# Block sums of an attention kernel taken from a second, unduplicated copy of the values

## The chip, the cores and the metric

The kernel runs on one core of a Trainium2 chip. Its time is device microseconds of one execution; a kernel's number is the median of its runs. Traces come from one profiled execution, whose own time is given beside its span.

## The reference

The program is an attention layer followed by a soft mixture of experts. Cut to what matters:

```python
# attention: B, H, S, D = 4, 8, 768, 64; blocks of 32, window 16
k_sum = k.reshape(B, H, nb, 32, D).max(axis=3)      # 24 block maxima of the keys
v_sum = v.reshape(B, H, nb, 32, D).mean(axis=3)     # 24 block means of the values
scores_l = scale * q @ k.T                          # kept where |i - j| < 16
scores_s = scale * q @ k_sum.T + log(32)
a = softmax(concat([scores_l, scores_s]))
x = (a @ concat([v, v_sum])).transpose(...)         # 3072 tokens x 512
# soft mixture: 8 experts, 4 slots each, hidden 1024
logits = x @ phi
slot_input = softmax(logits, over tokens).T @ x     # 32 slots
slot_out[e] = relu(slot_input[e] @ w1[e]) @ w2[e]
out = softmax(logits, over slots) @ slot_out
```

## The kernel before

**Steps.** Attention goes in 24 steps of 256 tokens and four heads: eight groups `hb` (a batch and half of its heads) of three steps each. A step has, in the order in which the program writes them: `norm` of the step before last, `scores` (TensorE, L253), `soft_max` (VectorE L271 adds the mask and takes the minimum, GpSimd L275 subtracts), then for the step before `trans` (TensorE, L286) and `evac` (ScalarE, L291), `soft_exp` (ScalarE, L280), and `values` (TensorE, L309). Every engine takes its instructions in this written order; the semaphores come from the tiles' reads and writes.

**Values with duplicates.** A value tile `v` holds, for each step, four stretches of 96 tokens that overlap by 32 with their neighbours, each with a column of ones; 24 of the 120 rows of a stretch are left free for the block sums. The host lays this out as `vx`; a tile is 520 KB, one a step, from a pool of five buffers, requested by `load_v` four steps ahead (the buffer comes free with `values` of the step before).

**Block sums.** `v_sum(hb)` adds up the values of a group's 24 blocks: 12 products (three tiles, four stretches) of a 120-row indicator (`cs` at `C_IND`) with 256 columns, into four column groups (32 rows each of a PSUM bank). Its further parts copy the sums to SBUF in two halves (L219, L220: a rounded part and the remainder), order them by a product with the selector `sel` (L224), and put them into `vsst` (L229), from where `put_v` (L235, GpSimd) writes them into each step's tile. `V0` to `V7` in the list `PLAN` say in which step each part of it is written; sum `hb` begins in step 3 `hb` (sum 0 in step 0).

**Maxima of the keys.** `k_max` (VectorE, L184) reduces the two key tiles of the next group in four parts: three in the step 3 `hb` + 1, one in the step after.

**Routing and experts.** The parts `X`, `L`, `t`, `D` of `PLAN` transpose x, form the logits, and accumulate the slot inputs, with a running maximum, beside later attention steps. After the last step the list `TAIL` finishes this: `R` combines the four lanes (with the tile `stk`, loaded for it late), `S` writes the slot inputs as `W1ST` (L449) and a reciprocal `rz` (L453, L454), `C1` takes the second part of the token-side softmax (L463 to L471). Then the attention's pools are closed; their eight PSUM banks (`ps_t` 2, `ps_o` 2, `ps_s` 2, `ps_p` 2) become `pf` (4) and `po` (4). The first expert product `hps` (L657) uses 32 weight pieces, the second (L690) another 32, with the output written beside it (L717 to L728).

**Loads.** All loads are issued by SyncE's queue, in written order; an issue waits for its buffer to be free, and for the landing of an earlier load that used the same semaphore. At the end of each step come: q for later steps, k two groups ahead, `LOADS[i]` weight pieces of 512 KB, `v` (from step 20 on the weights after `v`). 28 pieces have buffers of their own, 15 take over buffers of k, q, v and x as attention ends, 21 follow as the first product frees buffers.

Of the kernel before, what the change touches and what calls it, by code (L numbers as in the profile page):

```python
# [9 lines left out]
F32 = mybir.dt.float32  # L10
F32R = mybir.dt.float32r
# [5 lines left out]
B, H, S, D = 4, 8, 768, 64  # L17
NT, DM, NS, NE, DF = B * S, H * D, 32, 8, 1024
NB = S // 32
W = 96  # L20
U = W + NB
HB = 2 * B
TPS = 3
# [12 lines left out]

LOADS = [1, 1, 1, 2, 2, 1, 2, 1, 2, 1, 1, 2, 2, 1, 1, 1, 1, 2, 1, 2, 3, 2, 2, 1]


PLAN = {
# [38 lines left out]
def attention_soft_moe(  # L81
# [2 lines left out]
    kx: bass.AP,  # L84
    qx: bass.AP,
    vx: bass.AP,
    phi: bass.AP,
    w1: bass.AP,
    w2: bass.AP,
# [10 lines left out]
    wa = ctx.enter_context(tc.tile_pool(name="wa", bufs=NWA))  # L100
    kp = ctx.enter_context(tc.tile_pool(name="kp", bufs=4))
    qp = ctx.enter_context(tc.tile_pool(name="qp", bufs=2))
    vp_ = ctx.enter_context(tc.tile_pool(name="vp_", bufs=5))
    xs = ctx.enter_context(tc.tile_pool(name="xs", bufs=NX))
    att = ctx.enter_context(ExitStack())
    wk = att.enter_context(tc.tile_pool(name="wk", bufs=2, side="right"))
# [20 lines left out]
    pieces += [("w2", k) for k in range(32)]  # L127
    wt, slot = {}, {}

    order = ["wa"] * NWA + "vp kp kp vp xs qp vp vp kp kp vp xs xs xs xs".split()  # L130
    NPRE = len(order)

    def load_piece():
        k = len(slot)
        if k == len(pieces):
            return
        slot[k] = slot[k - NPRE] if k >= NPRE else order[k]
        pool = {"wa": wa, "kp": kp, "qp": qp, "vp": vp_, "xs": xs}[slot[k]]
        t = pool.tile([128, 1024], F32, name=f"w{k}", tag=slot[k])
        p = pieces[k]  # L140
        if p[0] == "w1":
            _, e, c = p
            nc.sync.dma_start(out=t, in_=w1[e, 128 * c : 128 * c + 128, :])
        else:
            nc.sync.dma_start(out=t, in_=w2[p[1]])
        wt[k] = t
# [18 lines left out]
    def load_v(i):  # L165
        if i < NSTEP:
            hb, tp = steps[i]
            v = vp_.tile([128, VC], F32, name=f"v{i}", tag="vp")
            nc.sync.dma_start(out=v, in_=vx[hb, tp])
            vt[i] = v.rearrange("p (a t h c) -> p a t h c", a=2, t=2, h=4)  # L170


    kst = {}


# [23 lines left out]

    def v_sum(hb):  # L200
        pv = post_bank()
        for tp in range(TPS):
            v = vt[hb * TPS + tp]
            for tt in range(2):
                for ab in range(2):
                    g = tt * 2 + ab
                    ic = C_IND + 36 * ab + 4 - 2 * tp
                    nc.tensor.matmul(  # L208
                        pv[32 * g : 32 * g + 32, 0:256],
                        lhsT=cs[0:U, ic : ic + 32],  # L210
                        rhs=v[0:U, ab, tt, :, 0:64],
                        start=(tp == 0),
                        stop=(tp == TPS - 1),
                        tile_position=(0, 32 * g),
                    )
        yield

        vp = wk.tile([128, 2, 256], F32R, name="vp", bufs=1)
        nc.scalar.copy(out=vp[:, 0], in_=pv[:, 0:256])  # L219
        nc.vector.tensor_tensor(out=vp[:, 1], in0=pv[:, 0:256], in1=vp[:, 0].bitcast(F32), op=ALU.subtract)  # L220
        yield
        pv = post_bank()
        for n in range(2):
            nc.tensor.matmul(pv[:, 0:256], lhsT=sel, rhs=vp[:, n], start=(n == 0), stop=(n == 1))  # L224
        yield
        n0 = VS[hb % 2]
        st = vsst[n0 : n0 + NB]
        src = pv[n0 : n0 + NB, 0:256].rearrange("p (h d) -> p h d", h=4)
        nc.scalar.copy(out=st[:, :, 0:64], in_=src)  # L229
# [189 lines left out]
    def lanes():  # L419
        pv = post_bank()  # L420
        pr = pv[0:1, 0:128].rearrange("p (g s) -> p g s", g=4)
        nc.tensor.transpose(pv[0:1, 0:128], stat[:, (NQ - 1) % 2 : (NQ - 1) % 2 + 1], ident)
        yield
        fg = wk.tile([1, 160], F32, name="fg", tag="vp", bufs=1)
        gm, f = fg[:, 128:160], fg[:, 0:128].rearrange("p (g s) -> p g s", g=4)
        nc.vector.tensor_reduce(out=gm, in_=pr.rearrange("p g s -> p s g"), axis=AX, op=ALU.min)
        nc.vector.tensor_tensor(out=f, in0=gm.unsqueeze(1).broadcast_to([1, 4, 32]), in1=pr, op=ALU.subtract)
        nc.scalar.activation(out=f, in_=f, func=AF.Exp)
        yield
        pc = post_bank()  # L430
        nc.tensor.matmul(pc[:, 0:1], lhsT=f.rearrange("p g s -> p (g s)"), rhs=one11, start=True, stop=True)
        yield
        R = wk.tile([128, 128], F32, name="R", tag="vp", bufs=1)
        nc.vector.tensor_scalar(out=R, in0=ps["stk"], scalar1=pc[:, 0:1], scalar2=None, op0=ALU.mult)
        ps["R"] = R
        yield
        pz = post_bank()
        nc.tensor.matmul(pz[:, 0:1], lhsT=R, rhs=stat[:, 2:3], start=True, stop=True)
        ps["z"] = pz
# [82 lines left out]
    nc.sync.dma_start(out=cs, in_=cst)  # L522
    self_ = wk.tile([128, 4, 128], F32, name="self_", tag="xt", bufs=4)[:, 0]
    nc.sync.dma_start(out=self_, in_=selx[0])
    for i in range(TPS):
        load_v(i)
    nc.sync.dma_start(out=phi_sb.rearrange("p c s -> p (c s)"), in_=phi)
    load_k(1)
    load_q(1)
    load_v(3)  # L530
    load_v(4)
    make_identity(nc, ident)
    nc.gpsimd.memset(vsst, 32.0)
    nc.gpsimd.memset(one11, 1.0)
# [5 lines left out]
    for i in range(NSTEP):  # L540
        j = i - 1
        before, after = PLAN.get(i, ("", ""))
        if j > 0:
            norm(j - 1)
        scores(i)
        if i == 1:
            parts("V0 V0")
            put_v(0, 1, nc.gpsimd)
        if i % TPS == 2 and i // TPS + 1 < HB:
            k_max(i // TPS + 1, 3)  # L550
        soft_max(i, 0)
        if i == 1:
            put_v(0, 0, nc.vector)
        if j >= 0:
            trans(j, 0)
            evac(j, 0)
            trans(j, 1)
            evac(j, 1)
            if i % TPS == 2 and i // TPS + 1 < HB:
                k_put(i // TPS + 1, nc.scalar.copy)  # L560
        else:
            for _ in range(3):
                nc.tensor.matmul(wm[:, 0:256], lhsT=acc[:, 0:128], rhs=acc[:, 0:256], start=True, stop=True)
        before, _, beside = before.partition("|")
        parts(before)
        soft_exp(i, 0)
        soft_max(i, 1)
        if i % TPS == 1 and i // TPS + 1 < HB:
            k_max(i // TPS + 1, 0, 1, 2)
        parts(beside)  # L570
        if j >= 0:
            values(j, 0)
            values(j, 1)
        soft_exp(i, 1)
        parts(after)
        if i > 0:
            put_v(i, 0, nc.gpsimd)
            put_v(i, 1, nc.gpsimd)
        if i % 2 == 1:
            load_q((i + 1) // 2 + 1)  # L580
        if i % TPS == 2:
            load_k(i // TPS + 2)
        for _ in range(LOADS[i] if i < 20 else 0):
            load_piece()
        if i > 0:
            load_v(i + 4)
        for _ in range(LOADS[i] if i >= 20 else 0):
            load_piece()
    j = NSTEP - 1
# [59 lines left out]

    row_split(0, 4)  # L650
    row_split(4, 2)
    hps = pf.tile([128, 512], F32, name="hps", tag="pf")[:, 0:256]
    for k in range(32):
        _, e, c = pieces[k]
        t = wt[k].rearrange("p (j f) -> p j f", j=4)
# [113 lines left out]
def _constants():  # L769
    cst = np.zeros((128, C_N), np.float32)  # L770
    i = np.arange(64)[:, None]
    j = np.arange(W)[None, :]
    band = (j - i >= 1) & (j - i <= 31)

    mask = np.zeros((2, 64, 4, U), np.float32)
    for n, ok in enumerate((band & (j >= 16), band, band, band & (j < 80))):
        ab = n // 2
        mask[:, :, n, np.where(np.arange(W) < S0[ab], np.arange(W), np.arange(W) + NB)] = np.where(ok, 0.0, NEG)
    cst[:, C_MASK:C_IND] = mask.reshape(128, 4 * U)

    ind = np.zeros((128, 2, 36), np.float32)
    for ab in range(2):
        for n in range(64):
            ind[16 + n + (NB if 16 + n >= S0[ab] else 0), ab, 4 + n // 32] = 1.0
    cst[:, C_IND : C_IND + 72] = ind.reshape(128, 72)
    sel = np.zeros((128, 128), np.float32)
    for n in range(NB):
        for n0 in VS:
            sel[32 * (n // 2 % 4) + 2 * (n // 8) + n % 2, n0 + n] = 1.0
    p = np.arange(128)  # L790
    stk = (p[:, None] % 32 == p[None, :] % 32).astype(np.float32)
    return cst, np.stack([sel, stk])
# [30 lines left out]
```

## Time and profile before

| | |
|---|---|
| median of 3 runs | 195.24 us (194.88 to 196.53) |
| the profiled execution | 194.91 us, span 193.1 us |
| granted TensorE clock, mean over the span | 0.973 |
| TensorE / VectorE / ScalarE / GpSimd busy | 88 / 60 / 48 / 41% of the span |
| moved by DMA | 67.64 MB, mean 350 GB/s |

A page of the profile gives busy time by engine, 40 slices of the span, the chain of work that ended last, followed back from the end, and groups of instructions by line. `out<-in` names the tiles of an instruction. PE is TensorE's matmuls, PEld its weight loads, DVE VectorE, ACT ScalarE, POOL GpSimd, SPq the queue on SyncE that issues loads. A line number is that of the kernel before.

### The profile page before, as it was taken

How to read it: one execution, taken by the hardware profiler on the slowest of the kernel's cores; microseconds unless marked ns; L12 is line 12 of the kernel's file. 1: busy time of each engine (PE TensorE's matmuls, PEld its weight loads, DVE VectorE, ACT ScalarE, POOL GpSimd, SP SyncE). 2: the span in 40 equal slices, each digit the busy share in tenths (PEclk: the TensorE clock that was granted, in tenths of full speed). 3: DMA queues.
4: the chain of work that ended last, by engine and by line, in shares of the span. 5: the costliest groups of instructions: out<-in, count | busy, mean ns of one | idle time of the engine just before them, and what ended most of it. 6: DMA issues, size and time to landing. Idle time of an engine off the chain costs nothing.

```text
span 193.1 us, 7825 instructions
## 1 busy us (share of the span) xinstructions
PE 169.9 (88%) x3163; PEld 128.7 (67%) x3163; DVE 115.1 (60%) x580; ACT 92.1 (48%) x202; POOL 78.7 (41%) x106
## 2 busy tenths in 40 slices
PE   7779899899799999799989999999879997889950
PEld 5537668677658778578856877876636667768720
DVE  2539959749629958868958867657573020143460
ACT  2036657658464775756686475847220031033440
POOL 2048766856645666576666465860010000000000
PEclk9999999999999999999999999999859999999996
DMA  6999999999998899999899976975959999987696
GB/s 211 351 415 418 416 414 417 419 415 413 404 416 342 277 398 418 410 377 354 247 395 392 392 236 238 311 267 204 333 193 316 417 420 415 416 319 303 259 393 260
DMA packets 19331, 67.64 MB, mean 350 GB/s; under 512 B 2144, under 2 KB 2528, under 8 KB 19296
## 3 DMA queue, kind: packets, MB, share of 16 engines
q1 hardware_dynamic: 19296, 67.15, 90.3%
q8 instruction: 25, 0.41, 0.8%
q14 instruction: 10, 0.08, 0.1%
HBM read 60.85 MB, written 6.29 MB: 348 GB/s over the span
## 4 chain that ended last, share of the span: by engine, by line
PE 60%; DVE 11%; issue 8%; DMA 8%; ACT 5%; POOL 3%; SPq 2%; POOLq 0%; ACTq 0%; DVEq 0%
PE o L309 9%; PE hps L657 8%; PE so L690 8%; DMA v<-vx 8%; PE pt L286 7%; PE s L253 6%; PE pp L208 5%; PE op L717 4%; DVE p L271 3%; DVE kh L184 3%; PE pp L399 2%; PE pp L356 2%; POOL p L275 2%; PE pp L340 2%; PE pp L224 1%
## 5 line engine op out<-in xcount | busy, mean ns | idle before, releaser
L275 POOL TENSOR_TENSOR p<-p,m 128x480 f32<-128x480 f32 x48 | 46.3, 986 | 23.3 <-DVE m L271 22.9
L271 DVE CUSTOM_DVE_ANT_0 p<-s,cs 128x120 f32<-128x120 f32 x192 | 41.0, 278 | 4.9 <-PE s L253 3.5
L280 ACT ACTIVATE p<-p 128x480 f32<-128x480 f32 x48 | 29.0, 608 | 21.8 <-POOL p L275 21.6
L235 POOL COPY v<-vsst 24x520 f32<-24x520 f32 x47 | 29.1, 620 | 20.2 <-issue 17.9
L291 ACT COPY ptr<-pt 120x512 f32<-120x512 f32 x48 | 26.5, 588 | 20.8 <-PE pt L286 20.3
L309 PEld LDWEIGHTS o<-v,ptr 120*64 120x64 f32 x736 | 24.0, 137 | 9.6 <-issue 4.1
L309 PE MATMUL o<-v,ptr 120*64 120x65 f32 x736 | 27.4, 225 | 1.7 <-issue 1.2
L286 PE MATMUL pt<-ident,p 128*120 128x128 f32 x192 | 27.3, 280 | 1.2 <-ACT p L280 1.1
L253 PE MATMUL s<-k,q 64*64 64x120 f32 x768 | 25.9, 269 | 2.1 <-DMA q<-qx 1.2
L253 PEld LDWEIGHTS s<-k,q 64*64 64x64 f32 x768 | 20.3, 133 | 6.1 <-issue 1.7
L286 PEld LDWEIGHTS pt<-ident,p 128*120 128x120 f32 x192 | 20.3, 137 | 6.0 <-ACT p L280 3.3
L184 DVE TENSOR_REDUCE kh<-k 128x30 f32<-128x480 f32 (+1 forms) x32 | 16.1, 545 | 3.4 <-DMA k<-kx 3.4
L657 PE MATMUL hps<-w,W1ST 128*32 128x256 f32 x256 | 15.8, 413 | 1.1 <-DVE lt_all L469 1.1
L329 DVE TENSOR_TENSOR x<-o,z 128x512 f32<-128x512 f32 x23 | 15.9, 691 | 0.8
L271 DVE DVE_READ_ACCUMULATOR2_ANT m<- 128x1 f32 x192 | 15.9, 83 | 0.0
L726 DVE COPY ot<-op 128x512 f32<-128x512 f32 x12 | 7.9, 688 | 11.6 <-PE op L717 11.6
L690 PE MATMUL so<-w,W1ST 128*32 128x128 f32 x256 | 13.4, 275 | 1.0 <-issue 1.0
L657 PEld LDWEIGHTS hps<-w,W1ST 128*32 128x32 f32 x256 | 9.2, 119 | 7.6 <-issue 3.1
L208 PE MATMUL pp<-v,cs 120*32 120x256 f32 x192 | 12.6, 384 | 1.9 <-DMA v<-vx 1.1
L690 PE MATMUL so<-w,W2ST 128*32 128x128 f32 x256 | 13.1, 273 | 0.0
L340 PE MATMUL pp<-ident,x 128*128 128x128 f32 x88 | 12.5, 274 | 0.3 <-ACT xt L346 0.3
L346 ACT COPY xt<-pp 128x512 f32<-128x512 f32 x21 | 12.1, 602 | 0.1
(112 smaller groups left out, 181.2 us busy)
## 6 DMA issues: line engine op xcount, KB each, us to landing
w<-w SPq DMA_DIRECT2D x64, 512.0 KB, 8.9
v<-vx SPq DMA_DIRECT2D x24, 520.0 KB, 7.7
k<-kx SPq DMA_DIRECT2D x16, 472.0 KB, 7.6
q<-qx SPq DMA_DIRECT2D x12, 512.0 KB, 7.0
out<-ot SPq DMA_DIRECT2D x10, 512.0 KB, 3.6
out<-ot SPq DMA_DIRECT2D x4, 256.0 KB, 3.4
cs<-cst SPq DMA_DIRECT2D x1, 288.0 KB, 6.2
self__116<-selx SPq DMA_DIRECT2D x1, 64.0 KB, 5.9
```

The source lines that it names most:

```text
L184: nc.vector.reduce_max(out=kh[:, pr, :, n0 : n0 + m], in_=v[:, :, c0 : c0 + 16 * m].rearrange("p j (m k) -> p j m k", k=16), axis=AX,)
L208: nc.tensor.matmul(pv[32 * g : 32 * g + 32, 0:256], lhsT=cs[0:U, ic : ic + 32], rhs=v[0:U, ab, tt, :, 0:64], start=(tp == 0), stop=(tp == ...
L235: eng.tensor_copy(out=v, in_=src)
L253: nc.tensor.matmul(ps_[i, ab][h : h + 64, u, :], lhsT=qt[i // 2][rows, c : c + 64], rhs=kt[hb, pr][rows, k0 : k0 + U], start=True, stop=Tr ...
L271: nc.vector.tensor_tensor_reduce(out=p[:, n, :], in0=ps_[i, ab][:, 2 * tt + pr, :], in1=maskv[:, mk, :], scale=-0.125, scalar=-NEG, op0=AL ...
L275: nc.gpsimd.tensor_tensor(out=p, in0=p, in1=m.unsqueeze(2).broadcast_to([128, 4, U]), op=ALU.subtract)
L280: nc.scalar.activation(out=p, in_=p, func=AF.Exp, scale=-1.0)
L286: nc.tensor.transpose(pt[:, n, :], p[:, n, :], ident)
L291: nc.scalar.copy(out=ptr, in_=ptr_[i, tt])
L309: nc.tensor.matmul(o[64 * ab : 64 * ab + 64, h, :], lhsT=ptr[:, 2 * pr + ab, 64 * (r ^ ab) : 64 * (r ^ ab) + 64], rhs=v[0:U, ab, tt, h, :] ...
L657: nc.tensor.matmul(hps[32 * j : 32 * j + 32, :], lhsT=W1ST[:, c, 28 * e : 28 * e + 32], rhs=t[:, j, :], start=(k == 0), stop=(k == 31), ti ...
L690: nc.tensor.matmul(so[32 * j : 32 * j + 32, :], lhsT=W2ST[i][:, j, 28 * e : 28 * e + 32], rhs=t[:, i, j, :], start=(e == 0 and i == 0), st ...
```

## The change

- The host adds `vox`, the values once, without overlap or ones: for each group six tiles of 128 tokens by 256 columns (four heads), 768 KB. It comes in beside `vx`, which stays.
- `v_sum` makes 6 products of 128 rows from it instead of 12: tiles 0 to 3 go to the four column groups, tiles 4 and 5 to the first two. The indicator is now one pattern of 128 rows; the selector's rows follow the new order of the sums.
- `load_vo(hb)` requests the copy: group 0 ahead of the first value tiles, group 1 in two halves in buffers of the x pool, groups 2 to 7 at the end of steps 3, 6, ..., 18, three steps ahead of their sum, in the single buffer of a new pool `vo`. The SBUF copy of the sums (`vp`) takes turns in the same buffer.
- The value pool has four buffers instead of five, and `v` is requested three steps ahead. `fg` and `R` of the tail take buffers of the softmax pool.
- At the start, the order of the loads after the first k, q and constants is now: copy 0, v 0, v 1, q 1, k of group 1, copy 1, v 2, v 3, phi.
- `LOADS` has 34 pieces instead of 36, and fewer of them early; some entries of `PLAN` move by a step (transposes `X4`, `X10` to `X15`, `D2`).
- `hps` takes its bank from `po`.

```diff
-LOADS = [1, 1, 1, 2, 2, 1, 2, 1, 2, 1, 1, 2, 2, 1, 1, 1, 1, 2, 1, 2, 3, 2, 2, 1]
+LOADS = [0, 0, 1, 1, 1, 1, 1, 2, 1, 1, 1, 1, 2, 1, 1, 1, 2, 1, 1, 2, 3, 4, 3, 2]
...
-    9: ("t0 t0 X4 X4 V3 | V3", "V3 V3 D0 D0"),
-    10: ("X5 X5", ""),
+    9: ("t0 t0 V3 | V3", "V3 V3 D0 D0"),
+    10: ("X4 X4 X5 X5", ""),
...
-    14: ("X9 X9 X10 X10 D1 | D1", ""),
+    14: ("X9 X9 D1 | D1", ""),
...
-    16: ("X11 X11", ""),
+    16: ("X10 X10 X11 X11", ""),
...
-    18: ("t2 t2 X12 X12 V6 | L2 V6", "V6 V6"),
-    19: ("X13 X13 X14 X14 D2 | D2", ""),
-    20: ("X15 X15", "L3 L3"),
+    18: ("t2 t2 V6 | L2 V6", "V6 V6 D2 D2"),
+    19: ("X12 X12 X13 X13", ""),
+    20: ("X14 X14 X15 X15", "L3 L3"),
...
-    vp_ = ctx.enter_context(tc.tile_pool(name="vp_", bufs=5))
+    vp_ = ctx.enter_context(tc.tile_pool(name="vp_", bufs=4))
+    vo = ctx.enter_context(tc.tile_pool(name="vo", bufs=1))
...
-    order = ["wa"] * NWA + "vp kp kp vp xs qp vp vp kp kp vp xs xs xs xs".split()
+    order = ["wa"] * NWA + "kp kp vp xs qp vp vp vo kp kp vp xs xs xs xs".split()
...
+    def load_vo(hb):
+        if hb == 1:
+            halves = [xs.tile([128, 1024], F32, name=f"vo1{n}", tag="xs")[:, 0:768] for n in range(2)]
+        elif hb < HB:
+            whole = vo.tile([128, 1536], F32, name=f"vo{hb}", tag="vo")
+            halves = [whole[:, 0:768], whole[:, 768:1536]]
+            nc.sync.dma_start(out=whole, in_=vox[hb])
+        if hb == 1:
+            for n in range(2):
+                nc.sync.dma_start(out=halves[n], in_=vox[hb, :, 768 * n : 768 * n + 768])
+        if hb < HB:
+            kst["vo", hb] = [halves[t // 3][:, 256 * (t % 3) : 256 * (t % 3) + 256] for t in range(6)]
...
     def v_sum(hb):
         pv = post_bank()
-        for tp in range(TPS):
-            v = vt[hb * TPS + tp]
-            for tt in range(2):
-                for ab in range(2):
-                    g = tt * 2 + ab
-                    ic = C_IND + 36 * ab + 4 - 2 * tp
-                    nc.tensor.matmul(
-                        pv[32 * g : 32 * g + 32, 0:256],
-                        lhsT=cs[0:U, ic : ic + 32],
-                        rhs=v[0:U, ab, tt, :, 0:64],
-                        start=(tp == 0),
-                        stop=(tp == TPS - 1),
-                        tile_position=(0, 32 * g),
-                    )
-        yield
-
-        vp = wk.tile([128, 2, 256], F32R, name="vp", bufs=1)
+        for t in range(6):
+            g = t % 4
+            ic = C_IND + 4 - 4 * (t // 4)
+            nc.tensor.matmul(
+                pv[32 * g : 32 * g + 32, 0:256],
+                lhsT=cs[:, ic : ic + 32],
+                rhs=kst["vo", hb][t],
+                start=(t < 4),
+                stop=(t + 4 > 5),
+                tile_position=(0, 32 * g),
+            )
+        yield
+
+        vp = vo.tile([128, 2, 256], F32R, name="vp", tag="vo")
...
-        fg = wk.tile([1, 160], F32, name="fg", tag="vp", bufs=1)
+        fg = wk.tile([1, 160], F32, name="fg", tag="p", bufs=3)
...
-        R = wk.tile([128, 128], F32, name="R", tag="vp", bufs=1)
+        R = wk.tile([128, 128], F32, name="R", tag="p", bufs=3)
...
-    for i in range(TPS):
-        load_v(i)
+    load_vo(0)
+    load_v(0)
+    load_v(1)
+    load_q(1)
+    load_k(1)
+    load_vo(1)
+    load_v(2)
+    load_v(3)
     nc.sync.dma_start(out=phi_sb.rearrange("p c s -> p (c s)"), in_=phi)
-    load_k(1)
-    load_q(1)
-    load_v(3)
-    load_v(4)
...
+        if i > 0 and i % TPS == 0:
+            load_vo(i // TPS + 1)
...
-            load_v(i + 4)
+            load_v(i + 3)
...
-    hps = pf.tile([128, 512], F32, name="hps", tag="pf")[:, 0:256]
+    hps = po.tile([128, 512], F32, name="hps", tag="op")[:, 0:256]
...
-    ind = np.zeros((128, 2, 36), np.float32)
-    for ab in range(2):
-        for n in range(64):
-            ind[16 + n + (NB if 16 + n >= S0[ab] else 0), ab, 4 + n // 32] = 1.0
-    cst[:, C_IND : C_IND + 72] = ind.reshape(128, 72)
+    cst[np.arange(128), C_IND + 4 + np.arange(128) // 32] = 1.0
...
-            sel[32 * (n // 2 % 4) + 2 * (n // 8) + n % 2, n0 + n] = 1.0
+            sel[32 * (n // 4 % 4) + 4 * (n // 16) + n % 4, n0 + n] = 1.0
```

More of the change, by code (lines that the diff above doesn't have):

```diff
@@ L86, in attention_soft_moe @@
     vx: bass.AP,
+    vox: bass.AP,
     phi: bass.AP,
@@ L137, in load_piece @@
         slot[k] = slot[k - NPRE] if k >= NPRE else order[k]
-        pool = {"wa": wa, "kp": kp, "qp": qp, "vp": vp_, "xs": xs}[slot[k]]
+        pool = {"wa": wa, "kp": kp, "qp": qp, "vp": vp_, "vo": vo, "xs": xs}[slot[k]]
         t = pool.tile([128, 1024], F32, name=f"w{k}", tag=slot[k])
@@ L805 @@
         "vx": vx,
+        "vox": np.ascontiguousarray(
+            inputs["v"].reshape(HB, 4, 6, 128, D).transpose(0, 3, 2, 1, 4).reshape(HB, 128, 6 * 256)
+        ),
         "phi": np.ascontiguousarray(inputs["moe_phi"].reshape(4, 128, NS).transpose(1, 0, 2).reshape(128, 4 * NS)),
```

## The prediction

> **What bounds the kernel now.** First the page: busy times, slices, and the chain of waits by engine and by line.
>
> ```profile
> span 193.1 us, 7825 instructions
> PE 169.9 (88%) x3163; PEld 128.7 (67%) x3163; DVE 115.1 (60%) x580; ACT 92.1 (48%) x202; POOL 78.7 (41%) x106
> ...
> GB/s 211 351 415 418 416 414 417 419 415 413 404 416 342 277 398 418 410 377 354 247 395 392 392 236 238 311 267 204 333 193 316 417 420 415 416 319 303 259 393 260
> ...
> PE 60%; DVE 11%; issue 8%; DMA 8%; ACT 5%; POOL 3%; SPq 2%; POOLq 0%; ACTq 0%; DVEq 0%
> PE o L309 9%; PE hps L657 8%; PE so L690 8%; DMA v<-vx 8%; PE pt L286 7%; PE s L253 6%; PE pp L208 5%; PE op L717 4%; DVE p L271 3%; DVE kh L184 3%; PE pp L399 2%; PE pp L356 2%; POOL p L275 2%; PE pp L340 2%; PE pp L224 1%
> ```
>
> TensorE is busy 88% of the span and makes 60% of the chain. L208, the block sums that are rewritten, is alone 5% of it, 9.7 us. Transfers are 8%, all of `v`; and from the third slice to the twelfth the queue moves 404 to 419 GB/s, which looks like its ceiling. Next the windows by stage (busy time of PE, PEld, DVE, ACT, POOL; then granted clock, DMA share, GB/s), and the chain in order of time (start us, us, what).
>
> ```profile
> 0.00:17.00 17.00, 13.04 (x150) 9.35 (x150) 8.02 (x44) 4.20 (x7) 5.04 (x13) 1.00 0.90 340
> 17.00:58.00 41.00, 36.55 (x721) 28.22 (x716) 28.69 (x171) 25.81 (x55) 26.61 (x35) 1.00 1.02 414
> 58.00:130.00 72.00, 68.93 (x1373) 55.03 (x1370) 55.38 (x310) 46.23 (x103) 46.05 (x59) 1.00 0.91 337
> 130.00:141.30 11.30, 9.03 (x93) 6.25 (x92) 7.95 (x25) 4.55 (x15) 0.00 (x0) 0.86 0.76 276
> 141.30:149.00 7.70, 7.66 (x109) 4.44 (x113) 4.18 (x10) 1.44 (x3) 0.95 (x1) 0.76 0.70 230
> ```
>
> ```profile
> 4.34 7.34 DMA v<-vx
> ...
> 17.26 7.60 DMA v<-vx
> 24.90 0.64 PE pp L208 x8
> ...
> 54.12 1.50 PE pp L208 x24
> ...
> 86.84 1.36 issue
> ...
> 114.57 1.43 PE pp L208 x24
> ...
> 141.34 15.82 PE hps L657 x256
> ```
>
> In the 72 us of steady attention TensorE is busy 96% and VectorE 77%, so I take TensorE as the bound there, and a matmul removed as time saved unless VectorE is next. The two `v` entries are the start (sum 0 wants three tiles) and step 3 (sum 1 wants tile 5, requested only when step 1 freed a buffer).
>
> **The change part by part.** *Sums 1 to 7.* One matmul of the source is two instructions, and four column groups run side by side. From the timeline:
>
> ```profile
> 10.16 0.64 PE L208 MATMUL pp<-v,cs 120*32 120x256 f32 x8
> ...
> 12.50 0.64 PE L208 MATMUL pp<-v,cs 120*32 120x256 f32 x8 [0.72 <-DMA v<-vx]
> ...
> 23.76 1.78 PE L208 MATMUL pp<-v,cs 120*32 120x256 f32 x24
> ```
>
> Eight instructions are two rounds of four groups and last 0.64 us; 24 are six rounds and last 1.50. A round is so (1.50 - 0.64) / 4 = 0.215 us. After, tiles 0 to 3 fill the four groups and tiles 4 and 5 come back to the first two: two rounds and two half-filled ones. I count a half-filled round as a whole one, since its group is busy as long; the bound on the other side is half the price. That is four rounds for six, 0.43 us saved in each of seven sums, 3.0 us (4.5 by the other bound). That the operand has 128 rows instead of 120 should cost nothing; L657's products of 128 rows and as many columns, 64 rounds in 15.82 us and partly at a slow clock, bound a round at 0.247, and the saving from below at 0.30 a sum, 2.1 us. Sum 1 also waited for tile 5: 1.78 against the usual 1.43, so 0.35 more. Where this goes to the end: the sums stand on the chain whole. But every third step VectorE has the maxima of k on top, and the chain's DVE, ACT and POOL entries (19%) show that an earlier TensorE is sometimes held there. I take 80% of 3.35, 2.7 us. The copy of the sums, its difference, the selection matmul and the put into the tiles stay as they are.
>
> *The start.* Ahead of sum 0 there were two k tiles, q, the constants, the selector and three v tiles; the page has the sizes, and the third tile's block began at 12.50.
>
> ```profile
> w<-w SPq DMA_DIRECT2D x64, 512.0 KB, 8.9
> v<-vx SPq DMA_DIRECT2D x24, 520.0 KB, 7.7
> k<-kx SPq DMA_DIRECT2D x16, 472.0 KB, 7.6
> q<-qx SPq DMA_DIRECT2D x12, 512.0 KB, 7.0
> ...
> cs<-cst SPq DMA_DIRECT2D x1, 288.0 KB, 6.2
> self__116<-selx SPq DMA_DIRECT2D x1, 64.0 KB, 5.9
> ```
>
> Now 768 KB of values stand for 1560: 792 KB less, 2.0 us at 414 GB/s, so sum 0 could begin at 10.5. It ends 0.64 + 2 x 0.215 = 1.07 later, at 11.6; before it ended at 13.14. That is 1.5 us. But the k tiles of the second head group slide back. Their second one and its reader:
>
> ```profile
> L157 SPq DMA_DIRECT2D k<-kx x1: 328/328/328, 7.6 to 7.6; - x1
> ...
> DMA to landing us min/median/max: 7.3/7.3/7.3
> ```
>
> ```profile
> 16.35 1.57 DVE L184 TENSOR_REDUCE kh<-k 128x30 f32<-128x480 f32 x3
> ```
>
> It landed at 7.6 + 7.3 = 14.9. Up to it the queue had 3368 + 64 + 944 = 4376 KB; after the change (sum's values, two v tiles, q, k) 5072, 696 KB more, 1.7 us: 16.6. The last of these three reductions needs it; about 0.6 us long, it ended at 17.92 and now cannot end before 17.2. VectorE is in order, and the next step's normalising and softmax queue behind. So the start brings 0.7 us; its bounds are 1.5 if the tile comes sooner, and -0.4 if the queue loses another microsecond, as its 340 GB/s up to 17 us would have it.
>
> *The queue.* Up to the tile `stk`, the last thing the routing tail needs from memory, the old program moves 16 k, 12 q, 24 v, 38 weight pieces and 480 KB of constants, 46,112 KB. The new one moves eight copies of 768 KB more and two pieces less: 51,232 KB, or 52.5 x 10^6 bytes. By 17 us 5.8 are there (340 x 17); the rest takes 112.8 us at 414 GB/s, and `stk` lands at 129.8. It is read at 137.45:
>
> ```profile
> L594 SPq DMA_DIRECT2D stk<-selx x1: 422/422/422, 127.4 to 127.4; - x1
> L434 DVE TENSOR_SCALAR R<-stk,pp x1: 291/291/291, 137.4 to 137.4; 128x128 f32<-128x128 f32 x1
> ```
>
> So the ceiling leaves 7.6 us of gain free at that point. The same for the k tiles of the last head group, which must come after 39.5 x 10^6 bytes: 98.5 at the earliest, against reductions that began at
>
> ```profile
> 104.80 1.57 DVE L184 TENSOR_REDUCE kh<-k 128x30 f32<-128x480 f32 x3
> ```
>
> With a gain of 3 us there it still fits, with about 3 us to spare, but the queue will be full almost throughout, so I charge 0.3 us for late tiles (bounds 0 and 2.5). The trace covers the other moves. Value tiles are asked for three steps ahead instead of four; steps last about 5 us, landing 7.7. The request of a copy waits on SP for the selection matmul of the same step, and behind it stand the weights and the v tile; v waited for the values product of that step already, and the selection follows it by under 1 us.
>
> By the Trainium skill (DMA: Bandwidth & Descriptors, Specifications) HBM gives one core about 358 GB/s; by that `stk` would land at 17 + 46.7 / 0.358 = 147 and the sum would come out near 204 us. The ten slices at 404 to 419 speak against it here.
>
> *The first expert product.*
>
> ```profile
> 139.46 0.29 DVE L449 COPY W1ST<-tl 128x128 f32<-128x128 f32 x1 [1.19 <-issue]
> ...
> 139.97 0.16 DVE L454 RECIPROCAL rz<-rz 128x1 f32<-128x1 f32 x1
> ...
> 140.77 0.42 DVE L469 TENSOR_TENSOR lt_all<-o,kh 128x256 f32<-128x256 f32 x1
> ...
> 141.34 1.93 PE L657 MATMUL hps<-w,W1ST 128*32 128x256 f32 x16 [1.07 <-DVE lt_all L469]
> ```
>
> Its weights are written at 139.75, but it waits for L469, which reads the banks of `ps_o`; the pool `pf` lies over them. In `po`, over `ps_s` and `ps_p`, the last readers are the `rz` lines, done by 140.13. That frees 1.07 us. The granted clock is 0.86 and 0.76 around this place, so the first part of the product is slow. If the slow phase ends when it ended before, an earlier microsecond does half a microsecond's work. I take 0.8 (bounds 0.5 and 1.1).
>
> By the Trainium skill (TensorE: Matmul & The Clock Gate, Part 1) the clock is released after a busy window of about 3.4 us on a grid that runs free of the kernel. By that the term is 0.5 unless the earlier start crosses a window's edge; the rows here show means of the clock and no edges.
>
> *The rest.* Some `X` parts move by a step, out of the steps of sums 3, 4 and 6, and `D2` moves from step 19 to the end of step 18. From the chain:
>
> ```profile
> 105.33 1.06 PE pp L399 x8
> ...
> 109.48 0.44 PE pp L340 x4
> ```
>
> Their number stays, so TensorE's sum does too; the copies of `X` (ScalarE) and the accumulation of `D2` (VectorE) go with them, and `D2` leaves a step with three k maxima on VectorE for one without. The parts `L` that read them are in a later step, except `L3`, which now follows `X14` and `X15` in one step where it followed `X15` alone. I count 0, bounds -0.4 and 0.7, one of these groups falling on or off the chain. `fg` and `R` take slots whose last readers are the transposes of steps 22 and 23, ten microseconds earlier: nothing. TensorE has 192 instructions fewer, which shifts its stalls without a shown cause (86.84, 1.36 us): I count 0, bounds plus and minus 1.4.
>
> Sum: 2.7 + 0.7 + 0.8 - 0.3 = 3.9 us. The profiled execution took 194.91, so 191.0; the median of the three runs, 195.24, is 0.33 above it: **191.3 us**, a case from 189.6 to 192.9.
>
> **The rivals.** *All of it counts*: 3.35 + 1.5 + 1.07 = 5.9, giving 189.3. For it: TensorE at 96%; against it: the late k tile. *VectorE or GpSimd is next in the sum's steps*, and only the start, the wait of sum 1 and half of the expert product remain: 0.7 + 0.35 + 0.5 = 1.6, giving 193.6. For it: the 19% of the chain; against it: the sums are on the chain in every step shown. *The queue becomes the bound, slower*: the place is `stk`, or a k or v tile before it. The point is the rate: 46.7 x 10^6 bytes in 137.45 - 17 us is 388 GB/s; below, routing waits. At 337, the mean of the second window, `stk` would land near 146, 8.7 late: 195.2 + 8.7 - 0.8 = 203; at 375, 199. Against it: that window's 337 is what was asked for, with slices of 418 and 410 in it. *The bank isn't free sooner* because the other pool is held as long: 0.8 less, 192.1.
>
> **How the numbers follow.** Forecast 0.50, all of it 0.13, VectorE next 0.21, queue 0.11, of which nearly all is slower, bank 0.05. The skill's 358 GB/s is in the queue's chance. About 1% is what a measurement of this kernel can tell (the three runs spread 0.8%). Faster by over 1%, below 193.3: 0.50 + 0.13 + 0.05 = 0.68; within 1%: 0.21; slower: 0.11. The range goes from 188.9 to 194.8; it leaves out the queue's case and the ends of the others.
>
> **What would show it.** Right: L208 in groups of 12 instructions of about 1.07 us; no wait of L208 for `v`; a VectorE wait for k near 15 to 17 us; over 400 GB/s up to about 100 us; the expert product about 0.2 us after `rz`. Wrong: `R`, the k maxima or the put waiting for a transfer after 20 us; steps as long as before with TensorE idle in front of VectorE; the slow clock lasting longer than before.

## The result and the profile after

The changed kernel takes 189.0 us in the median of four runs (187.4 to 189.9) against 195.1 beside it: ratio 0.970, interval 0.965 to 0.975, so 6.1 us less (5.8 by the ratio). On a second chip it was 187.7 against 194.9, ratio 0.963 (0.958 to 0.967). The forecast was 191.3, a gain of 3.9 us. The profiled execution took 187.42 us, the fastest of the four, against 194.91 in the trace before, so the two traces show 7.5 us, about 1.4 more than the medians. Executions also differ by stretches of 3.4 or 6.8 us at half clock that fall in different places, so below a ratio carries a time and a trace carries a wait.

Lines have moved by the change: L208 is now L221, L271 L284, L309 L322, L399 L412, L434 L447, L469 L482, L657 L674. The page, by the parts that were read before:

```profile
span 185.6 us, 7677 instructions
PE 167.0 (90%) x3067; PEld 126.1 (68%) x3067; DVE 114.9 (62%) x580; ACT 92.6 (50%) x202; POOL 78.8 (42%) x106
...
GB/s 208 380 416 415 415 415 423 413 419 406 415 415 427 413 411 378 410 418 419 413 419 419 412 418 417 417 417 414 417 402 391 416 414 420 417 410 366 238 422 256
...
PE 47%; DMA 28%; DVE 7%; POOL 7%; issue 5%; ACT 2%; SPq 0%; POOLq 0%; DVEq 0%
```

The windows of the same two stretches:

```profile
17.00:58.00 41.00, 37.39 (x720) 29.61 (x719) 31.28 (x190) 26.13 (x56) 26.92 (x35) 1.00 1.03 415
58.00:130.00 72.00, 69.04 (x1314) 53.91 (x1309) 56.49 (x304) 49.37 (x114) 44.27 (x56) 1.00 1.02 413
```

TensorE has lost 96 matmuls. The second stretch went from 337 to 413 GB/s: the queue now runs at its ceiling from the third slice to the thirty-sixth, 378 to 427 GB/s. DMA's share of the chain went from 8 to 28%. The parts of the forecast can be read in the timeline (first two rows) and in the chain (the others):

```profile
108.63 1.06 PE L221 MATMUL pp<-vo,cs 128*32 128x256 f32 x12
...
16.36 0.66 DVE L200 TENSOR_REDUCE kh<-k 128x30 f32<-128x480 f32 x1
```

```profile
123.58 8.94 DMA stk<-selx
...
132.62 0.30 DVE R L447
132.96 1.92 PE tl L458 x8
...
135.26 0.53 PE o L476 x2
135.78 15.55 PE hps L674 x256
```

A sum lasts 1.06 us (forecast 1.07). The last of the three reductions, which needs the late k tile, ends at 17.02 (forecast: not before 17.2; before the change 17.92). The expert product follows the transposes of `C1` with no wait. But `R` now stands behind the landing of `stk`, at 132.5, which the forecast had put at 129.8.

### The profile page after: what moved, and what is told of

It reads as the page before. It is cut to its first block, busy times and chain, and to the rows that moved or that the text cites. A ratio compares the mean times of both kernels' runs of the same rounds, so it can differ in the third digit from the quotient of the medians.

```text
span 185.6 us, 7677 instructions
## 1 busy us (share of the span) xinstructions
PE 167.0 (90%) x3067; PEld 126.1 (68%) x3067; DVE 114.9 (62%) x580; ACT 92.6 (50%) x202; POOL 78.8 (42%) x106
## 2 busy tenths in 40 slices
DMA packets 20626, 73.92 MB, mean 398 GB/s; under 512 B 2288, under 2 KB 2672, under 8 KB 20592
## 4 chain that ended last, share of the span: by engine, by line
PE 47%; DMA 28%; DVE 7%; POOL 7%; issue 5%; ACT 2%; SPq 0%; POOLq 0%; DVEq 0%
PE hps L674 8%; PE so L707 8%; DMA q<-qx 7%; DMA w<-w 6%; DMA v<-vx 6%; PE pt L299 5%; PE o L322 5%; PE s L266 5%; POOL p L288 5%; DMA stk<-selx 5%; DMA k<-kx 5%; PE op L734 4%; DVE p L284 2%; PE pp L353 2%; POOL v L248 2%
## 5 line engine op out<-in xcount | busy, mean ns | idle before, releaser
L284 DVE CUSTOM_DVE_ANT_0 p<-s,cs 128x120 f32<-128x120 f32 x192 | 41.1, 278 | 4.7 <-PE s L266 3.3
L322 PEld LDWEIGHTS o<-v,ptr 120*64 120x64 f32 x736 | 24.2, 137 | 11.0 <-issue 7.1
L322 PE MATMUL o<-v,ptr 120*64 120x65 f32 x736 | 27.9, 225 | 3.5 <-issue 2.5
L284 DVE DVE_READ_ACCUMULATOR2_ANT m<- 128x1 f32 x192 | 16.0, 83 | 0.0
L674 PE MATMUL hps<-w,W1ST 128*32 128x256 f32 x256 | 15.6, 409 | 0.0
L674 PEld LDWEIGHTS hps<-w,W1ST 128*32 128x32 f32 x256 | 8.2, 118 | 7.3 <-issue 2.1
L353 PEld LDWEIGHTS pp<-ident,x 128*128 128x128 f32 x88 | 10.0, 141 | 0.6 <-ACT xt L359 0.5
```

The costliest lines, as they stand in the source:

```text
L284: nc.vector.tensor_tensor_reduce(out=p[:, n, :], in0=ps_[i, ab][:, 2 * tt + pr, :], in1=maskv[:, mk, :], scale=-0.125, scalar=-NEG, op0=AL ...
L322: nc.tensor.matmul(o[64 * ab : 64 * ab + 64, h, :], lhsT=ptr[:, 2 * pr + ab, 64 * (r ^ ab) : 64 * (r ^ ab) + 64], rhs=v[0:U, ab, tt, h, :] ...
L353: nc.tensor.transpose(pv[:, 128 * c : 128 * c + 128], x, ident)
L674: nc.tensor.matmul(hps[32 * j : 32 * j + 32, :], lhsT=W1ST[:, c, 28 * e : 28 * e + 32], rhs=t[:, j, :], start=(k == 0), stop=(k == 31), ti ...
```

## Experiments

Each ran beside the kernel before on its chip, five rounds. Ratios are to that. The runs are spread over three chips, so kernels of different sets are compared by their ratios.

**1. Six rounds again.**

```diff
-        for t in range(6):
+        for n, t in enumerate((0, 1, 2, 3, 0, 1, 2, 3, 4, 5)):
...
-                stop=(t + 4 > 5),
+                stop=(n < 4 or t + 4 > 5),
```

> The changed kernel (189.0 us), but the first four products of each block sum are made twice, so that a sum takes six rounds of the four column groups again, as before the change; nothing else differs and the queue's loads are the same. TensorE theory (a round removed is time saved, 80% of 8 x 0.43 = 2.7 us): 191.7. Queue theory (the tail now waits 1.3 us for the tile stk, so the first 1.3 us of slower sums are hidden): 190.3. Hidden theory (VectorE and GpSimd set the steps with a sum): at most 189.4.

191.6 us, ratio 0.982 (0.977 to 0.988); the changed kernel has 0.970 and 0.963. Against these two numbers the run costs 2.4 and 3.9 us, each with about 1.5 us either way. The hidden theory falls. The other two are not told apart: TensorE's 2.7 fits both numbers, and the queue theory's 1.3 fits the first. The run doesn't price the rounds alone either, since its trace has more stalls of TensorE than the changed kernel's; they are counted below. The wait for `stk` is gone: `R` now waits for TensorE (second row; the first is the changed kernel on the second chip).

```profile
DVE R L447 <- DMA stk<-selx: 2.0, 1, 2.0
```

```profile
DVE R L447 <- PE pp L444: 0.2, 1, 0.2
```

But `stk` itself landed at 136.8 there (issued at 126.8, 10.0 later), 3 to 4 us after the two traces of the changed kernel: the requests of the copies wait for buffers that the steps free (SyncE waited 27.2 us for the selection product, against 21.4 and 18.2), so slower steps make the queue later too.

**2. The old PLAN in the changed kernel, and the new one in the old.** The diffs are the lines of `PLAN` shown with the change, taken back and put in.

> The changed kernel with the old PLAN: transposes X4, X10, X12 to X15 and D2 stand in their old steps. My forecast costs the moves at nothing: 189.0, within 0.4. Rival: steps 18 and 19 became 2.1 us shorter in the two traces, 0.43 of it the shorter sum; if the moves did the rest, 190.4 or more.

188.8 us, 0.967 (0.962 to 0.973): no difference, as the forecast had it. But in the kernel before:

> The kernel before (195.6 us on the last chip) with the new PLAN alone. Plan theory (two of the steps that lost a transpose or D2 get 1.3 us shorter each, as in the run with plan and bank): 193.0. Forecast (moves cost and bring nothing), so that the 4.4 us of plan and bank came from the bank and the clock behind it: 195.2 or more.

193.0 us, 0.989 (0.984 to 0.994). The moves alone bring 2.2 us (1.2 to 3.2). The list of waits of one line, L399, the product of a part `D`, says where to look. The kernel before, then with the new PLAN:

```profile
its engine sat idle before it (us, times) until:
  ACT xt L346: 3.3, 4
  ACT dsb L391: 0.9, 2
```

```profile
its engine sat idle before it (us, times) until:
  ACT dsb L391: 0.9, 2
  issue: 0.2, 1
```

The list adds up the waits of the matmuls and of their weight loads, which run at the same time; the matmuls alone have 1.4 of the 3.3 us:

```profile
PE pp L399 <- ACT xt L346: 1.4, 2, 1.0
```

Two parts `X` ahead of a `D` take both banks of `ps_p`, and `D` waits until ScalarE has copied one of them out. The timeline of step 14, before and with the new PLAN:

```profile
78.49 1.04 PE L340 MATMUL pp<-ident,x 128*128 128x128 f32 x8
80.55 1.07 PE L399 MATMUL pp<-x,dsb 128*32 128x512 f32 x8 [1.02 <-ACT xt L346]
```

```profile
78.22 0.60 PE L340 MATMUL pp<-ident,x 128*128 128x128 f32 x4
78.75 1.07 PE L399 MATMUL pp<-x,dsb 128*32 128x512 f32 x8
```

With one `X` there the wait of 1.02 us is gone, and the other of 0.4 in step 19 too. So 1.4 of the 2.2 us are seen in rows, within what the times allow; the rest is not accounted for. In the changed kernel with the old PLAN this wait is back, and yet costs nothing measurable (the two measurements of the changed kernel allow up to about 2 us). The trace of experiment 4, which has the old PLAN as well, shows it, and shows that `R` doesn't wait for `stk` there:

```profile
PE pp L412 <- ACT xt L359: 1.6, 2, 1.2
...
DVE R L447 <- PE pp L444: 0.2, 1, 0.2
```

**3. The bank.**

```diff
-    hps = po.tile([128, 512], F32, name="hps", tag="op")[:, 0:256]
+    hps = pf.tile([128, 512], F32, name="hps", tag="pf")[:, 0:256]
```

> The changed kernel with the first expert product in a bank of pf again. By the forecast's term it waits 1.1 us for L482 (the line that was L469) and costs 0.8 (0.5 to 1.1): 189.8. Rival: the slow clock of the product's first part ends at the same time and the product is behind the tile stk anyway: within 0.3 of 189.0.

189.3 us, 0.971 (0.966 to 0.977). The wait is back as foreseen:

```profile
PE hps L674 <- DVE lt_all L482: 1.2, 1, 1.2
```

The time lies between no change and 0.9% over the two measurements of the changed kernel: undecided between the two expectations. The reverse, in the kernel before:

> The kernel before with the first expert product in a bank of po, nothing else. The wait of 1.1 us goes: ratio 0.9945 to 0.9975 (1.1 to 0.5 us). Rival, plan and bank gave 3.9 us together and the moves 2.2, so the bank 1.7: 0.991.

193.9 us, 0.990 (0.981 to 0.999), and the wait of L657 is gone from its list. It brings something, between 0.3 and 3.7 us (the ratio rests on three of the six runs); whether 0.8 or 1.7 these runs can't tell. Both parts together, without the copy:

> The kernel before (195.1 us) with the two parts that need no copy of the values: the new PLAN and the bank in po; sums, loads and buffers are the old ones. My forecast: the bank alone, 0.8 us: 194.3. Rival, the moves of PLAN count 1.4 more: 192.9 or less.

191.3 us, 0.980 (0.974 to 0.986): 3.9 us, about the sum of the two, 2.2 and 1.9.

**4. The copy alone**, the changed kernel with the old PLAN and the old bank.

> The changed kernel with the old PLAN and the old bank: the copy, its sums, the new loads and buffers alone. Queue theory (what these two parts save is mostly spent waiting for the queue): ratio to before 0.970 to 0.975, about 190. Additive theory (moves 2.2 us and bank 1.1 go back in full from 0.966): 0.983, about 192.

189.4 us, 0.975 (0.969 to 0.981): 4.8 us, where the queue theory put it. The additive 0.983 lies just outside; but it starts from 0.966, between the changed kernel's 0.970 and 0.963, and from 0.963 it would be 0.980, inside. Moves 2.2, bank 1.9 and copy 4.8 make 8.9 us one by one; together they make 5.8 and 7.3 on the two chips. That would be 1.6 to 3.1 us lost where they meet, but the intervals add up to about 2.5 us either way, so the times alone don't show a loss. The traces do, under 5.

**5. A lighter queue.**

```diff
-            halves = [xs.tile([128, 1024], F32, name=f"vo1{n}", tag="xs")[:, 0:768] for n in range(2)]
+            halves = [xs.tile([128, 1024], F32, name=f"vo1{n}", tag="xs")[:, 0:768] for n in range(1)]
...
-            nc.sync.dma_start(out=whole, in_=vox[hb])
+            nc.sync.dma_start(out=whole[:, 0:256], in_=vox[hb, :, 0:256])
...
-            for n in range(2):
-                nc.sync.dma_start(out=halves[n], in_=vox[hb, :, 768 * n : 768 * n + 768])
+            nc.sync.dma_start(out=halves[0][:, 0:256], in_=vox[hb, :, 0:256])
...
-            kst["vo", hb] = [halves[t // 3][:, 256 * (t % 3) : 256 * (t % 3) + 256] for t in range(6)]
+            kst["vo", hb] = [halves[0][:, 0:256] for t in range(6)]
```

> The changed kernel with 128 KB of each copy loaded instead of 768 (all six products of a sum read the first 256 columns): left out are five sixths of the values that go into the block sums; instructions of the engines are the same, the queue has 5.2 x 10^6 bytes less, 12.7 us at 414 GB/s. Queue theory: no wait for stk (1.3) and none for the k tile at the start (0.8): 186.9, and 186 or less if a full queue also slows the steps between. Rival, the full queue costs nothing: 189.0 within 0.4.

184.6 us, 0.947 (0.942 to 0.952), against 187.7 for the changed kernel in the same set: 3.1 us (1.7 to 4.4 by the ratios), for the same instructions of the engines. Its two stretches:

```profile
17.00:58.00 41.00, 37.73 (x728) 29.75 (x731) 30.85 (x188) 26.46 (x57) 27.22 (x35) 1.00 0.98 378
58.00:130.00 72.00, 69.36 (x1318) 54.07 (x1318) 56.28 (x303) 49.36 (x115) 43.97 (x56) 1.00 0.99 388
```

The rival falls: the full queue costs something, by the medians 3.1 us, against the 1.3 and 0.8 that I could name. And if it is the queue that hides the moves of PLAN, they must show again here:

> The kernel with 128 KB copies (five sixths of the values left out of the block sums, 184.6 us on the last chip, ratio to before 0.947) with the old PLAN. Queue theory (with the whole copies the moves of PLAN are hidden behind the full queue; without the queue they are worth the 2.2 us that they are worth in the kernel before): ratio 0.958, 186.8. Rival (the shorter sums leave the moves nothing to gain): 0.947, 184.6 within 0.6.

186.3 us, 0.961 (0.954 to 0.967), 0.013 above the same kernel with the new PLAN, 2.6 us. Without the queue's load the moves are worth what they are worth in the kernel before, so the rival falls; with it, nothing measurable.

The traces show where the moves go. GpSimd subtracts twice in each step; the second of these rows is the changed kernel, the first the copy alone, with the old PLAN, both in the last step:

```profile
121.51 1.93 POOL L288 TENSOR_TENSOR p<-p,m 128x480 f32<-128x480 f32 x2 [0.69 <-DVE m L284]
118.56 1.93 POOL L288 TENSOR_TENSOR p<-p,m 128x480 f32<-128x480 f32 x2 [0.67 <-DVE m L284]
```

The same start in eight traces, with the start of `R` and the span (us):

| kernel of the trace | last subtractions | `R` | between | span |
|---|---|---|---|---|
| before | 124.53 | 137.45 | 12.92 | 193.1 |
| before, new PLAN | 122.25 | 135.18 | 12.93 | 191.5 |
| copy alone | 121.51 | 134.43 | 12.92 | 187.5 |
| changed | 118.56 | 132.62 | 14.06 | 185.6 |
| changed, second chip | 119.32 | 134.04 | 14.72 | 186.8 |
| changed, six rounds | 124.55 | 137.47 | 12.92 | 190.1 |
| light copies | 117.96 | 130.88 | 12.92 | 182.9 |
| light copies, old PLAN | 120.90 | 133.82 | 12.92 | 184.8 |

By the last step the moves have brought 2.3 us in the kernel before, 2.9 with the light queue, and 3.0 and 2.2 with the full one (copy alone against the two traces of the changed kernel; the bank, in which they differ too, acts behind `R`). So a full queue does not hide them in the steps. From there to `R` it is 12.9 us, except where `R` waits for `stk`: there 1.1 and 1.8 us are added, and of the moves 1.8 and 0.4 are left. In the copy's own trace `stk` landed at 133.7 and `R` began at 134.4: that was all the room that the moves could use. The six rounds show the same from the other side: 6.0 and 5.2 us later in the last step, 4.9 and 3.4 at `R`.

The same table says what the light queue saves. By the last step it is 0.6 and 1.4 us, and this was there by step 3 (0.8 and 1.3), after the k tile at the start, whose reductions end 0.8 us sooner than in the changed kernel:

```profile
14.65 1.57 DVE L199 TENSOR_REDUCE kh<-k 128x30 f32<-128x480 f32 x3
```

In the steps between, the full queue costs nothing in these traces. The wait for `stk` adds 1.1 and 1.8. Behind `R` another 1.0 and 0.7 remain. There TensorE's clock is at half for 3.4 us with the light copies and for 6.8 in both traces of the changed kernel, worth up to 1.7 us (half of the difference, an estimate). The mean granted clock over the runs agrees, 0.985 against 0.978. So a part of the 3.1 us may be the clock; that the queue causes this isn't shown.

**6. Towards a better version.** First the request of `stk` at the end of step 22:

```diff
+        if i == 22:
+            ps["stk"] = const.tile([128, 128], F32, name="stk", tag="sel")
+            nc.sync.dma_start(out=ps["stk"], in_=selx[1])
```

> The changed kernel with the request of the tile stk moved from behind the weights of the tail to the end of step 22, ahead of seven weight pieces. Queue theory (the tail waits 1.3 us for stk, since the queue is full to that point): stk lands some 8 us sooner, the wait goes, 187.7. Rival (something else in the tail is ready no sooner, or the slow clock gives it back): 189.0 within 0.4.

Beside it the changed kernel once more:

> The changed kernel once more, beside the next three on one chip: 189.0 again, within 0.8.

187.1 us, 0.957 (0.952 to 0.963), beside 187.7, 0.963. The wait of `R` for `stk` was 2.0 us in the second trace of the changed kernel and is gone here:

```profile
  DMA stk<-selx: 2.0, 1
```

```profile
  PE pp L444: 0.2, 1
```

From the last subtractions to `R` it is 12.9 us again (120.08 to 132.99). By the ratios the gain is 1.0 us, less than the wait, and the intervals overlap: not settled. Then the order of the first loads as well:

```diff
     load_v(0)
-    load_v(1)
     load_q(1)
     load_k(1)
+    load_v(1)
```

> The changed kernel with stk requested at the end of step 22, and at the start the second q tile and the two k tiles of group 1 ahead of the second value tile. The k tiles land 1.3 us sooner; VectorE waited 1.2 us for the second of them. Ratio to before 0.953 (stk alone 0.957), 186.0 to 186.5. Rival: the value tile is now late by as much, no gain: 0.957.

186.6 us, 0.961 (0.957 to 0.966), all six runs within 0.7 us. The wait of VectorE for k at the start is gone (first row: `stk` alone; second: with the new order; columns: total, times, longest). That wait was 0.5 us in the changed kernel, with another 0.2 before the reduction of the second tile, not 1.2, which is the time from the start of the first reduction to that of the third (15.19 to 16.36). By time it can't be told from `stk` alone (it ran on another chip).

```profile
DVE kh L200 <- DMA k<-kx: 3.2, 2, 2.7
```

```profile
DVE kh L200 <- DMA k<-kx: 2.6, 1, 2.6
```

Both versions have lower medians than the changed kernel, by 0.3 and 0.6%, and by the ratios 0.5 and 0.1%: neither is clear of the noise.

## Why the forecast was right, and where its size was off

The direction and the range held, and so did the first reason: TensorE was the bound of the steps, and rounds removed were time saved. The size was off, and that it lies as near as it does is partly luck: three terms were missed, and one of them has the other sign. The measured 6.1 lies on the rival in which all terms count (5.9), but not for its reasons: that one had full shares for start and sums, and neither the moves, the stalls nor the queue at their real size.

- *Sums*: 1.06 us each against 1.07, so the row was right. What share of it reaches the end (80% in the forecast) was not measured: experiment 1's 2.4 to 3.9 us hold stalls besides the rounds, and what `R` hides.
- *Start*: the late k tile landed at about 16.4 (issued at 7.5, 8.9 later), forecast 16.6; the reductions ended 0.9 us sooner than before, forecast 0.7. Right, and by its own limit: 1.5 was there for the sum, and VectorE's wait for k took the rest.

```profile
L159 SPq DMA_DIRECT2D k<-kx x1: 328/328/328, 7.5 to 7.5; - x1
...
DMA to landing us min/median/max: 8.9/8.9/8.9
```

- *Expert product*: the wait went as described. Of its 0.8 us the runs leave 0.3 to 3.7; the half-clock argument could not be decided.
- *Moves of PLAN*: costed at nothing, with a bound of 0.7. They measured 2.2 us in the kernel before and 2.6 with a light queue. This is the first mis-sized term. The sum counted their instructions, which stay, and looked at VectorE; it didn't look at what the moved lines wait for. In the old trace the waits of L399's matmuls for ScalarE's copies of `X`, 1.4 us, named the larger part of the price.
- *Stalls of TensorE*: counted at nothing, with a bound of 1.4. "Issue" in the list of waits is idle time for which the profile shows no releaser. TensorE's matmuls before, then after:

```profile
PE pp L356 <- issue: 1.8, 1, 1.8
PE op L717 <- issue: 1.3, 1, 1.3
PE o L309 <- issue: 1.2, 2, 0.8
PE so L690 <- issue: 1.0, 1, 1.0
```

```profile
PE o L322 <- issue: 2.5, 4, 1.0
PE so L707 <- issue: 0.8, 1, 0.8
PE s L266 <- issue: 0.2, 1, 0.2
```

  With 0.2 more at L253 the trace before has 5.5 us of them, the changed kernel's two have 3.5 and 2.5: 2 to 3 us less. It isn't one execution's luck. The four traces with the old sums have 5.5 to 6.8, each with 1.8 to 2.0 at L356 and 1.3 to 1.8 at L717; the nine with the new sums have 2.3 to 3.8 and nothing at these two places; the one with six rounds, which has 64 matmuls more, has 5.3. So the stalls go with the program. Why they come, and what they are worth in time, no run here shows.
- *Queue*: charged at 0.3 with a bound of 2.5. By the light copies its cost is 3.1, of which 0.8 is the k tile, already in the start's term: so 2.3, the clock's part included; the wait for `stk` alone is 1.1 to 1.8. The ceiling was right (414 forecast, 415 and 413 measured), and the bytes moved rose from 67.64 to 73.92 MB, the eight copies. But `stk` landed at 132.5, not 129.8. And the 7.6 us of room were measured against the old time of `R`: as every other term brought `R` forward, it ate its own room. `R` was ready 6.1 us sooner (132.62 less the wait of 1.3, against 137.45) and `stk` came 2.7 later than forecast: 8.8 against 7.6. In the rival of the slower queue the two rates stand on different footings: 337 was put on the second stretch alone, 375 on everything behind 17 us. `R` waiting for a transfer stood on the forecast's list of signs against it, and it did come.

So the forecast missed about 2.2 us of gain by the moves, 2 to 3 us of stalls that went, and 2 us of cost by the queue. Moves and queue largely cancel in the changed kernel; what is left, 2.2 us of 195, is the size of the stalls that went. That the terms add up so is an account from single traces, not a measurement of each. The 358 GB/s of the Trainium skill (DMA: Bandwidth & Descriptors, Specifications) did not bind: 413 GB/s as a mean over 72 us.

What stays open: the cause of the stalls; the bank's share, 0.3 to 3.7 us; and why the clock falls to half for 3.4 us with the light copies and for 6.8 with the whole ones.

## What to carry to other kernels

A part that is moved costs what it waits for, not only what it does: before costing a reordering at nothing, read the waits of every moved line, and count the buffers that the lines ahead of it hold. When a change spends a resource with slack, like a queue at 337 of 415 GB/s, measure the slack against the new time of the consumer, since every other gain shrinks it. Where several edits come together, their gains add only until the next bound: here the moves were worth 2.2 to 3.0 us in the last step and 0.4 to 1.8 behind the wait for `stk`. Two starts on different engines, read in every trace, show where a gain is lost better than the times do. And a change in the number of instructions can move stalls that have no releaser: count them over several traces before taking them as they were.

## What was not expected of the hardware

TensorE's clock falls to half for stretches of 3.4 or 6.8 us, one or two of the windows that the Trainium skill describes (TensorE: Matmul & The Clock Gate, Part 1); the lengths agree. What I had not expected is that place and number change so much between traces of nearly one program. In windows laid on them (granted clock is the third number from the end), the changed kernel, then the light copies, then the changed kernel with the old PLAN:

```profile
132.20:139.00 6.80, 6.04 (x44) 4.00 (x48) 4.21 (x12) 0.42 (x1) 0.95 (x1) 0.50 1.02 408
```

```profile
132.40:135.80 3.40, 3.40 (x31) 1.59 (x35) 2.97 (x9) 0.42 (x1) 0.95 (x1) 0.50 1.00 358
```

```profile
18.00:21.50 3.50, 1.27 (x35) 1.04 (x33) 2.80 (x12) 1.45 (x4) 0.25 (x1) 1.00 1.03 415
21.50:28.30 6.80, 5.76 (x57) 3.77 (x52) 3.88 (x29) 2.88 (x5) 5.14 (x6) 0.50 1.02 415
```

The last has it near the start, behind 3.5 us in which TensorE was busy 1.27; that execution took 192.6 us, 3.8 more than its kernel's median. The program with six rounds has none before the end of its span. Half the clock over 3.4 to 6.8 us is worth up to 1.7 to 3.4 us (half the stretch, an estimate), as much as most of the edits here.
